# Fewer filler matmuls in the prologue, one shared ring for the mixed inputs, and a fourth output buffer

## The chip, the cores and the metric

The kernel runs on one core of a Trainium2 chip. Times are device microseconds of one execution. Eight runs of the kernel before gave 412.10 to 415.53 us, with a median of 412.3 us. A profile is one further execution, recorded by the hardware profiler; all readings of engines, waits and transfers below come from it.

## The reference

Two layers follow each other. The first is a causal convolution along the sequence with 7 taps per head (8 heads of 24 channels, taps from a softmax). The second is a channel mix: each position is blended with the position before it, in two ways, and the blends go through matrices.

```python
# x: (8, 4160, 192), weight: (8, 7)
w = softmax(weight, axis=-1)                       # per head
y = sum over k of w[h, k] * x_padded[s + k]        # causal, pad 6 zeros in front
y_prev = y shifted by one position
xk = mu_k * y + (1 - mu_k) * y_prev
xr = mu_r * y + (1 - mu_r) * y_prev
k = relu(xk @ w_k)                                 # (.., 1024)
v = (k * k) @ w_v                                  # (.., 192)
out = sigmoid(xr @ w_r) * v                        # float32
```

## The kernel before

The eight sequences are worked on in four pairs; 64 channels of one sequence and 64 of the other fill the 128 partitions. A pair's positions are cut into steps, mostly of 512 positions (three steps of 256 at the very start, one of 256 at the end of the first pair, and one that collects the tails of all pairs). Each step of 512 has eight "slots" of K work. Four slots make a bundle, and a bundle is the unit of the order, which is written out by hand: `manual_schedule` keeps the instructions of each engine as the Python code issues them.

**Prologue** (lines 824 to 867). The taps' weights are loaded and put through a softmax on ScalarE and VectorE; the first block of x comes in through two hardware queues into `x_f` and is cast into `xb`; GpSimd issues the other loads of x and of the matrices. TensorE meanwhile runs matmuls whose results nobody reads: `SHORT` = 85 matmuls of one column (line 851), three of 512 columns (line 822, `WARM[0]`), then, after the eight small matmuls of the taps (line 254), two more of 512 columns. The first useful convolution matmuls follow at line 413 (`conv_t`), as soon as `xb` is cast.

**First bundles** (`bundle_first`, `bundle_second`, `bundle_third`). These turn the convolution of the first positions straight into the transposed layout `yT`, while K's matmuls for the three short steps start. The order on TensorE is: 168 matmuls of line 413, four slots of K (line 593), one slot, and then, between more slots and convolutions, slots 4 and 5 of the short steps. The third bundle begins with K's matmuls for two slots, followed by R's (line 650) and V's (line 681).

**Steady state** (`bundle_rest`). In each bundle TensorE computes four K slots, R for 256 positions and V for 256 positions, and a convolution unit for later positions. ScalarE applies the relu (line 605) and the sigmoid (line 661) out of PSUM, VectorE squares K (line 619), forms the difference `d` (line 536), scales and adds it into `xk` and `xr` (lines 567 and 573, function `scale`, `add_y`, `mix`) and multiplies V by R into `o_sb` (line 697, `v_out`). SyncE issues two stores per `o_sb`, and the writes and transposing reads of `y`.

**Buffers.** A tile pool gives each tag a ring of buffers. A tile takes a buffer that is free, and its first writer waits for the last reader of the tile that held it. K's inputs `xk` and R's inputs `xr` have three buffers each, of 128 partitions by 3 x 512 bf16; `o_sb` has three of 128 by 768 float32; `k_sb` has four. PSUM is one ring of four tiles of two banks.

In a step of 512, whose slots fill bundles f and f+1, `xk` is first written in bundle f-1 and last read by the last slot of bundle f+1; `xr` is first written late in bundle f-1 and last read by R's second half in bundle f+3.

The built program has 15,465 TensorE instructions in a row, a weight load and a matmul each for 7,718 matmuls and a few others; the TensorE has no loop.

Of the kernel before, what the change touches and what calls it, by code (L numbers as in the profile page):

```python
# [7 lines left out]
FP32 = mybir.dt.float32  # L8
BF16 = mybir.dt.bfloat16
# [5 lines left out]
def kernel(  # L15
# [13 lines left out]
    B, S, D = x.shape  # L29
# [3 lines left out]
    P = 128  # L33
    NF = DF // P
    Q = 64
    NC = D // Q
# [8 lines left out]
    STEP = 512  # L45
# [1 line left out]
    NPAIR = B // 2  # L47
    YC = 16
    WARM = (3, 2)
    SHORT = 85  # L50

    const = ctx.enter_context(tc.tile_pool(name="const", bufs=1))
    two = ctx.enter_context(tc.tile_pool(name="two", bufs=2))
    three = ctx.enter_context(tc.tile_pool(name="three", bufs=3))
    four = ctx.enter_context(tc.tile_pool(name="four", bufs=4))
    ring = ctx.enter_context(tc.tile_pool(name="ring", bufs=4, space=bass.MemoryType.PSUM))
    dram = ctx.enter_context(tc.tile_pool(name="dram", bufs=1, space=bass.MemoryType.DRAM))

# [457 lines left out]
    diffs, xks, xrs = {}, {}, {}  # L516
# [5 lines left out]
    def y_of(s, cs, k):  # L522

        p, t0, L, _, _ = steps[s]
        if s == LAST:
            return y_tail[:, cs, :, k : k + TAIL, :].rearrange("p c a t b -> p c a (t b)")
        return yTs[p][:, cs, YC + t0 - 1 + k : YC + t0 - 1 + k + L]
# [12 lines left out]
    def mix(s, i, sl=slice(0, NC)):  # L540

        L = steps[s][2]
        d = diffs[s]
        if s < 2 and i == 0:
            if sl.start == 0:
                xks[s] = three.tile([P, NC, STEP], BF16, tag="xk", name="xk")
            t = xks[s]
            c = sl.start
            nc.vector.scalar_tensor_tensor(  # L549
                out=t[:, c, :L],  # L550
                in0=d[:, c, :L],
                scalar=mu[:, i, c : c + 1],
                in1=y_of(s, sl, 0)[:, 0, :],
                op0=ALU.mult,
                op1=ALU.add,
            )
            return
        scale(s, i, *range(sl.start, sl.stop))
        add_y(s, i, sl)

    def scale(s, i, *cs):
        L = steps[s][2]
        if s not in (xks, xrs)[i]:
            (xks, xrs)[i][s] = three.tile([P, NC, STEP], BF16, tag=("xk", "xr")[i], name=("xk", "xr")[i])
        t = (xks, xrs)[i][s]
        for c in cs:
            nc.vector.tensor_scalar(  # L567
                out=t[:, c, :L], in0=diffs[s][:, c, :L], scalar1=mu[:, i, c : c + 1], scalar2=None, op0=ALU.mult
            )

    def add_y(s, i, sl=slice(0, NC)):
        o = shaped(s, (xks, xrs)[i][s][:, sl, : steps[s][2]])
        nc.vector.tensor_tensor(out=o, in0=o, in1=y_of(s, sl, 0), op=ALU.add)  # L573
# [57 lines left out]
    def v_mm(o, s, t):  # L631
        for f in range(NF):
            nc.tensor.matmul(  # L633
                out=o,
                lhsT=k2s[s][:, f, t * P : (t + 1) * P],
                rhs=wv[:, f, :],
                start=(f == 0),
                stop=(f == NF - 1),
            )
# [51 lines left out]
    def tile_of(s, j, k):  # L691
        return k // 2 * (steps[s][2] // P) + 2 * j + k % 2

    def v_out(s, j):
        p, t0, L, _, _ = steps[s]
        o_sb = three.tile([P, 4, D], FP32, tag="o_sb", name="o_sb")
        nc.vector.tensor_tensor(  # L697
            out=o_sb.rearrange("p (b t) d -> p b (t d)", b=2),
            in0=v_ps.pop((s, j)),
            in1=r_sbs.pop((s, j)),  # L700
            op=ALU.mult,
        )
        for st in range(2):
            c = t0 + 2 * j * P
            nc.sync.dma_start(
                out=out[2 * p + st, c : c + 2 * P, :].rearrange("(m p) d -> p m d", p=P),
                in_=o_sb[:, 2 * st : 2 * st + 2, :],
            )

    def v_last(s, j):  # L710

        r_sb = r_sbs.pop((s, j))
        o_sb = three.tile([P, 4, D], FP32, tag="o_sb", name="o_sb")
        for k in range(4):
            ps = ring.tile([P, 2, BANK], FP32, tag="k", name="ps_v")
            v_mm(ps[:, 0, 0:D], s, tile_of(s, j, k))
            nc.vector.tensor_tensor(
                out=o_sb[:, k, :],
                in0=ps[:, 0, 0:D],
                in1=r_sb[:, k // 2, k % 2 * D : (k % 2 + 1) * D],  # L720
                op=ALU.mult,
            )
            (nc.scalar if k % 2 else nc.sync).dma_start(
                out=bass.AP(
                    tensor=out.tensor,
                    offset=out.offset + ((4 * (k % 2) + k // 2) * S + T0) * D,
                    ap=[[D, TAIL], [2 * S * D, 2], [1, D]],
                ),
                in_=o_sb[:, k, :],
            )  # L730
# [49 lines left out]
    for s, (p, t0, L, n0, ns) in enumerate(steps):  # L780
        fb = first_bundle[s]
        if s == 0:
            at(mix_a, 1, mix, s, 1)
            continue
        if s < 3:
            at(late, s + 1, mix, s, 1)
        else:
            if s == 3:
                at(mix_c, 1, diff, s)
            elif s == 5:  # L790
                at(mix_b, fb - 1, diff, s)
            else:
                at(mix_c, fb - 2, diff, s)
            at(mix_b if s == 5 else mix_a, fb - 1, scale, s, 0, 0)
            at(mix_b, fb - 1, scale, s, 0, 1, 2)
            at(mix_c, fb - 1, add_y, s, 0)
            if s == 3:
                at(mix_a, fb, scale, s, 1, 0)
                at(mix_b, fb, scale, s, 1, 1)
            else:  # L800
                at(mix_c, fb - 1, scale, s, 1, 0)
                at(mix_a, fb, scale, s, 1, 1)
            at(mix_b, fb, scale, s, 1, 2)
            at(mix_b, fb, add_y, s, 1)
        if s == LAST - 1 or s < LAST and steps[s + 1][0] > p:
            at(late, fb - 1, keep_tail, p)
# [17 lines left out]
    def prologue():  # L824
# [23 lines left out]

        for i in range(SHORT):
            q = slice(i % 4 * 32, i % 4 * 32 + 32)  # L850
# [18 lines left out]
    def bundle_first(ns):  # L869
        new_yT(0)  # L870
        tiles = [ring.tile([P, 2, BANK], FP32, tag="k", name="ps_t") for _ in range(2)]
        for n, (g, c) in enumerate((g, c) for g in range(2) for c in range(NC)):
            o = tiles[n % 2][:, n // 2 % 2, :]
            conv_t(g, c, o, range(groups[g][2]))
            if n == 0:
                turn_mu()
            to_yT(g, c, o, 0, groups[g][2], nc.scalar.copy)
            if g == 0:
                diff(0, slice(c, c + 1))
                if c == 0:  # L880
                    nc.vector.tensor_copy(out=mu.rearrange("p i c -> p (i c)"), in_=warm_ps[:, 1, 0 : 2 * NC])
                mix(0, 0, slice(c, c + 1))

        for c in range(NC):
            diff(1, slice(c, c + 1))
            mix(1, 0, slice(c, c + 1))
        diff(2)
        mix(2, 0)
        for n in ns:
            k_mm(n)  # L890
            k_relu(n)
        for n in ns:
            k_square(n)
        run(late, 0)
# [32 lines left out]
    def bundle_rest(b, ns):  # L927
# [3 lines left out]
        if b == 3:  # L931
            for n in range(2):
                k_mm(ns[n])
                k_relu(ns[n])
            tr(3, 0)
            tr(3, 1)
            k_square(bundles[b - 1][3])
            for u in xt[b - 1]:
                conv_tiles(*u)
                conv_tiles_out(*u)  # L940
            run(mix_a, b)
        else:
            if b == 4:
                v_out(*vq[b - 1][0])
            k_square(bundles[b - 1][3])
            run(mix_a, b)
            if b > 4:
                v_out(*vq[b - 1][0])
            for n in range(2):
                k_mm(ns[n])  # L950
                k_relu(ns[n])
# [26 lines left out]
    def bundle_third(b, ns):  # L978

        quad = vq[b][0]  # L980
        for n in bundles[b - 1][2:]:
            k_square(n)
        run(mix_a, b)
        k_mm(ns[0])
        k_relu(ns[0])
        k_square(ns[0])
        k_mm(ns[1])
        k_relu(ns[1])
        run(rq, b)
        run(rs, b)  # L990
        v_rows(*quad, 0)
        conv_out(*xt[b - 1][1], nc.scalar.copy)
        k_square(ns[1])
        run(mix_b, b)
        run(mix_c, b)
        run(late, b)
        k_mm(ns[2])
        k_relu(ns[2])
        v_rows(*quad, 1, (0,))
        k_mm(ns[3])  # L1000
        k_relu(ns[3])
        v_rows(*quad, 1, (1,))
        v_out(*quad)
        k_square(ns[2])
# [56 lines left out]
```

## Time and profile before

| what | value |
|---|---|
| median of 8 runs | 412.3 us |
| profiled execution's own time | 412.14 us |
| its span, first to last instruction | 410.4 us |
| TensorE busy (matmuls) | 401.4 us, 98% |
| VectorE busy | 372.2 us, 91% |
| ScalarE busy | 354.6 us, 86% |
| share of TensorE in the chain that ended last | 93% |
| packets of the instruction queue q8 | 60, 0.98 MB together |

Busy time of TensorE comes from records whose ends are modelled, so that matmuls in a row overlap in the records; idle time before a group is the safer reading. "PEld" is TensorE loading weights, "issue" is time in which an engine waited for nothing that the profile shows. In the rows of the chain of waits the columns are the start in microseconds, the length and what ran; in those of groups by line they are the line, the engine, the operation, the tiles, shapes and count, then busy time, the mean time of one in nanoseconds, and the idle time ahead of it with what ended it. In the rows of waits, the total, the number of times and the longest are given. In the rows of queues the number of packets, the megabytes and the share of 16 engines are given.

### The profile page before, as it was taken

What the parts mean: (1) busy time and instruction counts of PE and PEld (TensorE: products, weight loads), DVE (VectorE), ACT (ScalarE), POOL (GpSimd) and SP (SyncE); (2) the same over time, 40 slices, a digit from 0 to 9 for tenths busy, and PEclk for the clock granted to TensorE, in tenths of its full rate; (3) what the DMA queues carried; (4) which work ended last, traced back from release to release, by engine and by line L of the source; (5) the groups of instructions that cost most, each with busy time, mean ns of one, the idle gap of its engine ahead of it and who ended that gap; (6) DMA issues with size and microseconds to landing.
All of it is one profiled execution on the core that took longest, in us unless ns stands there. A gap on an engine that the chain in (4) does not pass through costs nothing.

```text
span 410.4 us, 17521 instructions
## 1 busy us (share of the span) xinstructions
PE 401.4 (98%) x7718; PEld 304.6 (74%) x7718; DVE 372.2 (91%) x680; ACT 354.6 (86%) x426; POOL 58.1 (14%) x91
## 2 busy tenths in 40 slices
PE   7889999999999999999999999999999999999996
PEld 5676777777877777767777777777777778777795
DVE  5989899998989999989999999999999899999973
ACT  6888988898998789988898998889898878887781
POOL 8623023030051003204020022100000001000000
PEclk9999999999999999999999999999999999999999
DMA  8999889998569997999995996968633846221223
GB/s 144 191 201 188 180 192 213 238 200 211 133 106 221 203 235 122 217 221 179 217 134 152 241 158 143 171 166 207 126 94 85 214 134 156 81 68 50 80 78 117
DMA packets 139124, 66.36 MB, mean 162 GB/s; under 512 B 89364, under 2 KB 139048, under 8 KB 139048
## 3 DMA queue, kind: packets, MB, share of 16 engines
q1 hardware_dynamic: 95704, 48.32, 46.7%
q0 software_dynamic: 42544, 16.36, 34.6%
q8 instruction: 60, 0.98, 1.0%
q10 hardware_dynamic: 800, 0.57, 0.5%
q14 instruction: 16, 0.13, 0.1%
HBM read 33.29 MB, written 36.99 MB: 171 GB/s over the span
## 4 chain that ended last, share of the span: by engine, by line
PE 93%; DVE 4%; DMA 1%; issue 1%; ACT 1%; ACTq 0%
PE ps_v L681 41%; PE ps_k L593 39%; PE ps_r L650 8%; PE ps_c L364 2%; PE ps_v L633 1%; PE ps_t L413 1%; DVE k L619 1%; DMA x_f<-in_x_dram 1%; PE ps_c L319 1%; DVE d L536 1%; DVE xr L567 0%; DVE xk L549 0%; DVE yT L511 0%; PE ps_c L393 0%; ACT k_sb L605 0%
## 5 line engine op out<-in xcount | busy, mean ns | idle before, releaser
L605 ACT ACTIVATE k_sb<-ps_k 128x1024 bf16<-128x1024 f32 x260 | 253.3, 1040 | 35.1 <-PE ps_k L593 34.7
L619 DVE TENSOR_TENSOR k<-k_sb 128x1024 bf16<-128x1024 bf16 x260 | 173.2, 686 | 25.1 <-ACT k_sb L605 25.0
L593 PE MATMUL ps_k<-xk,wk 64*128 64x512 bf16 (+1 forms) x1680 | 192.0, 361 | 2.0 <-issue 1.1
L681 PE MATMUL ps_v<-wv,k 64*128 64x192 bf16 x4032 | 188.4, 243 | 0.0
L681 PEld LDWEIGHTS <-k 64*128 64x128 bf16 x4032 | 168.4, 94 | 12.0 <-issue 4.5
L593 PEld LDWEIGHTS <-wk 64*128 64x128 bf16 x1680 | 85.4, 94 | 56.6 <-issue 2.4
L154 POOL DMA_DIRECT2D xb<-in_x_dram x62 | 43.9, 716 | 143.6 <-DVE xb L125 59.6
L697 DVE TENSOR_TENSOR o_sb<-ps_v,r_sb 128x768 f32<-128x768 f32 x64 | 60.8, 950 | 2.6 <-issue 2.4
L661 ACT ACTIVATE r_sb<-ps_r 128x768 bf16<-128x768 f32 x65 | 53.7, 827 | 8.8 <-PE ps_v L681 7.2
L337 ACT CAST y<-ps_c 128x960 bf16<-128x960 f32 (+2 forms) x84 | 52.6, 709 | 0.0
L650 PEld LDWEIGHTS <-xr 64*128 64x128 bf16 x780 | 34.8, 94 | 14.6 <-issue 0.7
L650 PE MATMUL ps_r<-wr,xr 64*128 64x192 bf16 x780 | 43.2, 243 | 0.5 <-DVE o_sb L697 0.5
L567 DVE TENSOR_SCALAR xr<-d,mu 128x512 bf16<-128x512 bf16 (+1 forms) x105 | 35.4, 343 | 0.0
L567 DVE TENSOR_SCALAR xk<-d,mu 128x512 bf16<-128x512 bf16 (+1 forms) x99 | 32.7, 365 | 0.1
L536 DVE TENSOR_TENSOR d<-yT 128x1536 bf16<-128x1536 bf16 (+2 forms) x38 | 31.5, 829 | 1.3 <-ACT yT L423 1.2
L573 DVE TENSOR_TENSOR xr<-xr,yT 128x1536 bf16<-128x1536 bf16 (+1 forms) x34 | 31.2, 918 | 1.2
L573 DVE TENSOR_TENSOR xk<-xk,yT 128x1536 bf16<-128x1536 bf16 (+1 forms) x32 | 29.9, 934 | 0.1
L520 POOL COPY y_tail<-yT 128x195 bf16<-128x195 bf16 x4 | 3.4, 844 | 89.5 <-DMA yT<-y_dram 89.5
L364 PEld LDWEIGHTS <-toe 32*32 32x32 bf16 x640 | 4.4, 87 | 8.6 <-issue 7.4
L364 PE MATMUL ps_c<-xb,toe 32*32 32x240 bf16 x640 | 9.3, 267 | 0.0
L127 POOL MEMSET xb<- 32x384 bf16 x3 | 1.2, 408 | 55.2 <-DVE xb L125 48.6
L413 PEld LDWEIGHTS <-xb 128*32 128x32 bf16 (+3 forms) x264 | 4.9, 113 | 2.1 <-ACT xb L247 1.3
(58 smaller groups left out, 66.8 us busy)
## 6 DMA issues: line engine op xcount, KB each, us to landing
out_dram<-o_sb SPq DMA_DIRECT2D x128, 192.0 KB
xb<-in_x_dram POOLq DMA_DIRECT2D x52, 240.0 KB, 8.0
y_dram<-y SPq DMA_DIRECT2D x40, 195.0 KB
y_dram<-y SPq DMA_DIRECT2D x16, 210.0 KB
xb<-in_x_dram POOLq DMA_DIRECT2D x4, 228.0 KB, 5.0
xb<-in_x_dram POOLq DMA_DIRECT2D x4, 192.0 KB, 6.2
wk<-in_moe_w_k_dram POOLq DMA_DIRECT2D x4, 192.0 KB, 6.7
xb<-in_x_dram POOLq DMA_DIRECT2D x2, 216.0 KB, 4.8
```

The costliest lines, as they stand in the source:

```text
L154: nc.gpsimd.dma_start(out=xb[q0 : q0 + rows, lo:hi, s, :], in_=bass.AP(tensor=x.tensor, offset=x.offset + (b * S + t0 + lo * step) * D, ap ...
L337: nc.scalar.copy(out=bass.AP(tensor=y.tensor, offset=y.offset + d, ap=[y.ap[0], [m * 2 * D, 2], [2 * D, m], [Q, 2], [1, b - a]],), in_=bas ...
L536: nc.vector.tensor_tensor(out=shaped(s, diffs[s][:, cs, :L]), in0=y_of(s, cs, 1), in1=y_of(s, cs, 0), op=ALU.subtract)
L567: nc.vector.tensor_scalar(out=t[:, c, :L], in0=diffs[s][:, c, :L], scalar1=mu[:, i, c : c + 1], scalar2=None, op0=ALU.mult)
L573: nc.vector.tensor_tensor(out=o, in0=o, in1=y_of(s, sl, 0), op=ALU.add)
L593: nc.tensor.matmul(out=ps[:, i, f * L : (f + 1) * L], lhsT=wk[r, c, fs], rhs=xk[r, c, :L], start=c == 0 and f == 0, stop=c == NC - 1 and f ...
L605: nc.scalar.activation(out=k_sb, in_=ps.rearrange("p a b -> p (a b)"), func=AF.Relu)
L619: nc.vector.tensor_tensor(out=o, in0=i, in1=i, op=ALU.mult)
L650: nc.tensor.matmul(out=ps[:, i, k * D : (k + 1) * D], lhsT=xr[q, c, ts], rhs=wr[q, c, :], start=c == 0, stop=c == NC - 1,)
L661: nc.scalar.activation(out=r_sbs[s, j], in_=r_ps.pop((s, j))[:, :, 0 : 2 * D], func=AF.Sigmoid)
L681: nc.tensor.matmul(out=v_ps[s, j][:, bank, k * D : (k + 1) * D], lhsT=k2s[s][q, f, t * P : (t + 1) * P], rhs=wv[q, f, :], start=half == 0 ...
L697: nc.vector.tensor_tensor(out=o_sb.rearrange("p (b t) d -> p b (t d)", b=2), in0=v_ps.pop((s, j)), in1=r_sbs.pop((s, j)), op=ALU.mult,)
```

## The change

`SHORT` goes from 85 to 60. The tags `xk` and `xr`, three buffers each, become one tag `xkr` with five. `o_sb` moves from a ring of three to a ring of four. The pool with five buffers is new.

```diff
-    SHORT = 85
+    SHORT = 60
...
+    five = ctx.enter_context(tc.tile_pool(name="five", bufs=5))
...
-                xks[s] = three.tile([P, NC, STEP], BF16, tag="xk", name="xk")
+                xks[s] = five.tile([P, NC, STEP], BF16, tag="xkr", name="xk")
...
-            (xks, xrs)[i][s] = three.tile([P, NC, STEP], BF16, tag=("xk", "xr")[i], name=("xk", "xr")[i])
+            (xks, xrs)[i][s] = five.tile([P, NC, STEP], BF16, tag="xkr", name=("xk", "xr")[i])
...
     def v_out(s, j):
-        o_sb = three.tile([P, 4, D], FP32, tag="o_sb", name="o_sb")
+        o_sb = four.tile([P, 4, D], FP32, tag="o_sb", name="o_sb")
...
     def v_last(s, j):
-        o_sb = three.tile([P, 4, D], FP32, tag="o_sb", name="o_sb")
+        o_sb = four.tile([P, 4, D], FP32, tag="o_sb", name="o_sb")
```

As built, TensorE has 50 instructions fewer (25 weight loads and 25 matmuls of line 851), and 15,415 in all. The order of everything else is the same on all five engines. On VectorE three waits of the mix differ. The first `xk` of a step of 512 no longer waits for TensorE; the `xr` of the second short step (written in the third bundle) and the first `xk` of the second pair now do. The waits of `o_sb` for stores name the store four tiles back instead of three.

## The prediction

> **What bounds the kernel now.** I read the engines' busy time first, then the chain of waits, then the groups that the edits touch, and last the instruction queue's packets.
>
> ```profile
> PE 401.4 (98%) x7718; PEld 304.6 (74%) x7718; DVE 372.2 (91%) x680; ACT 354.6 (86%) x426; POOL 58.1 (14%) x91
> PE 93%; DVE 4%; DMA 1%; issue 1%; ACT 1%; ACTq 0%
> ```
>
> TensorE bounds the span: it is 93% of the chain that ended last. Nearly all of VectorE's 4% lies before 38 us. So an edit is worth what it takes from TensorE's idle time or, ahead of 38 us, from this chain:
>
> ```profile
> 9.25 0.57 ACT yT L423
> 9.84 0.30 DVE d L536
> ...
> 18.12 0.76 PE ps_k L593 x12
> ...
> 20.24 0.11 PE ps_k L593 x2
> 20.35 1.07 issue
> 21.42 1.38 PE ps_k L593 x22
> ```
>
> One piece is odd: TensorE stands still for 1.07 us from 20.35 inside a slot of K, between two matmuls with the same operands, for "issue". It is the largest such piece in the chain. Now the prologue on TensorE:
>
> ```profile
> 1.53 0.83 PE L851 MATMUL warm<-ones_t 128*32 128x1 bf16 x85 [1.53 <-DVE ones_t L830]
> 2.30 1.46 PE L822 MATMUL warm<-zeros,ones_t 128*128 128x512 bf16 x3
> 4.23 0.35 PE L254 MATMUL w_ps<-w_tap,tap 8*128 8x8 bf16 x8 [0.47 <-DVE w_tap L252]
> 4.52 1.03 PE L822 MATMUL warm<-zeros,ones_t 128*128 128x512 bf16 x2
> 5.93 0.79 PE L413 MATMUL ps_t<-toe,xb 128*32 128x120 bf16 x24 [0.38 <-ACT xb L247]
> ```
>
> The 85 fillers end at 2.30; the taps' matmuls wait for VectorE until 4.23 and the convolution for ScalarE's cast until 5.93. VectorE's waits for its output tile over the whole run, and two queues in one microsecond ahead of the stall:
>
> ```profile
> DVE o_sb L697 <- issue: 2.4, 1, 2.4
> ...
> DVE o_sb L697 <- PE ps_v L681: 0.2, 1, 0.2
> ```
>
> ```profile
> q0 software_dynamic: 490, 0.18, 154.1%
> q8 instruction: 1, 0.02, 6.1%
> ```
>
> The last two are the window 18.5 to 19.5 us: q0, GpSimd's loads, takes the engines more than whole, and one instruction packet is among them. The page counts 60 such packets with 0.98 MB, 16,384 bytes each in the packet records, for 15,465 TensorE instructions: 256 instructions each (60 x 256 = 15,360). Counted in the built program, exactly 961 instructions stand before the idle's end. The first four packets start at 4.93, 12.76, 18.95 and 25.41 and take 0.94 to 0.97. So I read the idle as a wait for code: with blocks that begin at instructions 193, 449, 705, 961, 1217 and so on, the packet at 18.95 lands at 19.92 and the block runs at 21.42, 1.5 later. Each packet is asked for when the block before it is entered; at quiet times it starts 1.1 to 1.25 after the instruction some 60 places ahead of that entry has begun.
>
> **The change part by part.** The sum is made against the profiled execution's 412.14 (span 410.4, 1.7 around it), 0.16 under the median of 412.3.
>
> *The 25 matmuls.* 0.77 us for 85 (1.53 to 2.30) is 9 ns each, so 25 x 9 = 0.23 us. It is hidden: the taps' matmuls still wait for `w_tap` at 4.23, so the idle of 0.47 ahead of them becomes 0.70. Value 0. Cover gone would cost at most 0.23.
>
> *The ring of five.* In steady state a first write of `xk` finds live the last `xk`, the last `xr` and the `xr` before, then adds `xk` and `xr`: five. So none waits. The wait taken away (first `xk` of a step of 512, at 22.14) had VectorE busy until it: 0 gained. The two added waits are for the last slot of the second bundle (TensorE at 18.05 to 18.9, writer at 26.28) and for reads of the bundle before, which VectorE's square of that bundle's last slot has already outwaited. Behind a wait there would stand `k_square`, then the V matmuls. Value 0; bounds: VectorE's idle before the `xk` and `xr` rows, 0.0 and 0.1, below, and one slot of K, 1.3 (27.20 row, 12 matmuls of 109 ns), above.
>
> *The fourth output buffer.* `o_sb` has one idle of 2.4 at its first use, where no store has been issued, and 0.2 for TensorE. Nothing waits for stores. Value 0, at most 0.2 gained.
>
> *The 50 instructions fewer.* This moves all 59 block entries 50 instructions, 25 matmuls, later in the work. Nothing else of the change touches TensorE's path, so it carries the forecast. In the numbering of before, entries come at 243, 499, 755, 1011, 1267.
>
> First the chain that sets 961 today. Entry 449 is foreseen at 8.67; packet at 12.76 (4.1 later), usable 0.97 + 1.48 later at 15.2; that sets off the packet at 18.95 (3.75 later), usable at 21.42; that one the packet at 25.41 (3.99), usable at 27.85, when 1217 runs with nothing to spare. So in this stretch of full q0 a block needs 6.2 to 6.5 us, and TensorE is held at this pace.
>
> After: entry 499 is foreseen at 9.28 instead of 8.67. If its own block is there by then, 9.28 + 6.5 = 15.8 (755 is reached at 16.1), + 6.2 = 22.0 for 1011, which ran at 22.72 before: 0.7 gained. Had the delay been nothing, 1.07 would be.
>
> But is the block of 499 there? Its packet is asked for by entry 243, foreseen 60 places ahead, at the taps' matmuls: 3.7 to 4.2, against 2.0 today. Today's started 2.9 after. The nearest rows for one with q0 active are 3.75 to 4.1. I take 3.4, halfway: 4.0 + 3.4 + 0.95 + 1.5 = 9.85. That is 0.55 after 9.28, so the chain slips: 16.4, 22.55 for 1011, and 0.16 gained. Ends: 3.7 + 2.9 + 2.4 = 9.0 (0.7 gained, at most 1.07) and 4.2 + 4.1 + 2.4 = 10.7 (0.7 lost).
>
> *The other 55 entries.* Without stall today, but two of them with under 0.5 us to spare (at 71.5 and 163.1). Drawing the delays of like places for the moved entries gives 0.2 lost on average, 0 to 0.7 in most draws. I take 0.2.
>
> Sum: 412.14 + 0 + 0 + 0 - 0.16 + 0.2 = 412.2.
>
> [...]
>
> **The rivals.**
>
> *The stall goes.* If the first packet is early, 0.7 to 1.07 is gained and no other entry stalls: 411.1 to 411.4. For it: q0 begins only at 4.0, so little may stand ahead of the packet. Against it: all saturated rows.
>
> *The first packet comes late, slower than before.* If the foreseeing stops at an instruction that waits, entry 243 is only seen after 5.93, when `xb` is cast (four instructions of the convolution's first 24 stand at 6.0 to 6.5). Then 6.1 + 3.9 + 2.4 = 12.4 for 499, 18.9 for 755, 25.1 for 1011, against 22.72: +2.4, 414.5. It decides by over 0.3% once block 499 is usable after 11.2 (9.28 + 0.7 + 1.24). Against it: today's first packet starts 0.7 after the wait at 4.23 ends, less than the 1.1 of any quiet one, so it was asked for before.
>
> [...]
>
> *It does nothing.* The stall only moves and keeps its 1.07: 412.1, in my range anyhow.
>
> **How the numbers follow.** The likeliest (stall kept in part, 411.5 to 413.0) has 0.55. The stall gone has 0.20; with luck at other entries a part of it passes 0.3%, which is 1.24 us and about what a measurement of this kernel can tell from no change. The late packet has 0.15, its smaller versions among them; the clock 0.05; several late stalls at other entries, each up to 1 us, 0.05. Faster by over 0.3% (under 411.06): 0.12. Slower (over 413.54): 0.22, from the last three less their small cases. Same: 0.66. The range runs from 410.9, the whole stall gone and 0.2 more, to 414.2, most of the late packet's case.
>
> **What would show it.** Right: `o_sb`, `xk` and `xr` rows without new idle; line 851's group ends near 2.08 with 0.7 idle ahead of line 254; the "issue" piece of 20.35 is gone from its place, and one stands, if any, in R's matmuls of line 650 (instruction 1011) near 21.5, shorter than 1.07; the first q8 packet starts near 7.4. Wrong: an "issue" idle of over 0.5 near 10 us in line 413, or the first packet after 9; "issue" in later bundles at block edges; line 413 slow beyond 9.4.

## The result: 0.5% slower, and the profile after

The changed kernel takes 414.94 us (median of 25 runs, 413.54 to 417.37) against 412.83 us (67 runs): a ratio of 1.0051, 95% interval 1.0041 to 1.0061, or 2.1 us. Forecast were 412.2 us and "same". The profiled execution took 413.86 us, near the low end of the 25, with a span of 412.1 us: 1.7 over the profile before.

The page of the changed kernel, busy time of the engines and the chain that ended last, looks much as it did:

```profile
PE 402.5 (98%) x7693; PEld 305.6 (74%) x7693; DVE 372.7 (90%) x680; ACT 354.9 (86%) x426; POOL 59.1 (14%) x91
PE 92%; DVE 2%; issue 0%; ACTq 0%
```

This chain reaches back only to 21.2 us, so it does not hold the stretch that the forecast was about. I went there. TensorE's instructions of the changed kernel in order of time (start, length, line, tiles, count, and in brackets the idle ahead and what ended it):

```profile
1.53 0.62 PE L852 MATMUL warm<-ones_t 128*32 128x1 bf16 x60 [1.53 <-DVE ones_t L831]
2.09 1.46 PE L823 MATMUL warm<-zeros,ones_t 128*128 128x512 bf16 x3
4.24 0.36 PE L255 MATMUL w_ps<-w_tap,tap 8*128 8x8 bf16 x8 [0.69 <-DVE w_tap L253]
...
5.55 0.79 PE L414 MATMUL ps_t<-toe,xb 128*32 128x120 bf16 x24
...
6.47 3.35 PE L414 MATMUL ps_t<-toe,xb 128*32 128x120 bf16 x124
11.85 0.44 PE L414 MATMUL ps_t<-toe,xb 128*16 128x120 bf16 x20 [2.03 <-issue]
12.21 5.77 PE L594 MATMUL ps_k<-xk,wk 64*128 64x256 bf16 x72
17.91 1.02 PE L414 MATMUL ps_t<-toe,xb 128*32 128x120 bf16 x64
...
24.59 0.58 PE L651 MATMUL ps_r<-wr,xr 64*128 64x192 bf16 x9 [0.78 <-issue]
```

All lines are one higher than before, for the line that the new pool adds. The fillers' part went as forecast: 0.62 us for 60, and 0.69 idle ahead of the taps. New is an idle of 2.03 us for "issue" inside line 414, where TensorE's chain of 168 convolution matmuls had run unbroken. It ends at instruction 449 of the built program, 256 after 193, the first edge of a block of code. The idle of 1.07 us at 20.35 is gone; in its place, at instruction 961 again but 25 matmuls later in the work, stands one of 0.78.

The queues say why. From 4.5 to 9.5 us, the kernel before and then the changed one (packets, megabytes, share of 16 engines):

```profile
q0 software_dynamic: 1339, 0.71, 111.9%
q8 instruction: 1, 0.02, 1.2%
```

```profile
q0 software_dynamic: 1302, 0.70, 117.3%
q1 hardware_dynamic: 13, 0.00, 0.4%
```

GpSimd issues the same loads; the instruction packet is missing from the second. In the packet records it starts at 9.54 instead of 4.93 and ends at 10.51, and its block runs at 11.85. From there the edges follow each other much as before, one per 5.6 to 6.7 us:

| edge, instruction | reached, before | idle there | reached, changed | idle there |
|---|---|---|---|---|
| 449 | 9.39 | none | 11.85 | 2.03 |
| 705 | 15.80 | none | 18.40 | none |
| 961 | 21.42 | 1.07 | 24.59 | 0.78 |
| 1217 | 27.85 | none | 31.25 | none |

The changed kernel's edges stand 25 matmuls later in the work, so its 24.59 compares with 22.72 before: 1.87 late. The first V matmuls of the third bundle come at 24.93 instead of 23.25, and the last group of all at 402.89 instead of 401.15: 1.68 and 1.74. Little is lost or won between. The stretch of 345 us from 43.3 before and from 45.0 now shows the same work on every engine, 6,534 and 6,533 matmuls. So this pair of profiles accounts for 1.7 of the 2.1 us between the medians.

The idle is followed by half clock. Windows of the changed kernel, three, and then the middle one of the kernel before. After the busy time and count of the five engines come the clock that TensorE was granted, the busy share of the DMA engines and GB/s:

```profile
9.40:12.70 3.30, 1.27 (x53) 0.92 (x44) 1.54 (x5) 0.95 (x3) 2.65 (x5) 1.00 1.42 177
12.80:16.10 3.30, 3.30 (x36) 2.38 (x32) 3.08 (x8) 2.50 (x4) 2.69 (x4) 0.50 1.46 198
16.20:19.60 3.40, 3.40 (x108) 2.70 (x104) 3.07 (x6) 3.37 (x4) 0.71 (x1) 0.99 1.59 187
```

```profile
12.80:16.10 3.30, 2.98 (x77) 2.29 (x75) 3.27 (x8) 3.30 (x5) 2.63 (x4) 1.00 1.45 190
```

In 9.40 to 12.70 TensorE was busy 1.27 of 3.30 us; in the next window it was granted half its clock. K's matmuls there take 398 ns instead of 269:

```profile
L594 PE MATMUL ps_k<-xk,wk 64*128 64x256 bf16 x36 | 3.8, 398 | 0.0
```

In this execution that costs little by itself: the block of the next edge was usable at about 18.1 (the packet's end at 16.72 and 1.4), and TensorE came to it at 18.40, so some 0.3 us. Nor would an earlier packet alone have gained anything here: at half clock TensorE would still have come to the edge at 18.40. The late block and the half clock lie on top of each other at this edge.

### The profile page after: what moved, and what is told of

The parts are those of the page before. It is cut to its first block, busy times and chain, and to the rows that moved or that the text cites. A ratio compares the mean times of both kernels' runs of the same rounds, so it can differ in the third digit from the quotient of the medians.

```text
span 412.1 us, 17469 instructions
## 1 busy us (share of the span) xinstructions
PE 402.5 (98%) x7693; PEld 305.6 (74%) x7693; DVE 372.7 (90%) x680; ACT 354.9 (86%) x426; POOL 59.1 (14%) x91
## 4 chain that ended last, share of the span: by engine, by line
PE 92%; DVE 2%; issue 0%; ACTq 0%
PE ps_v L682 40%; PE ps_k L594 39%; PE ps_r L651 8%; PE ps_c L365 2%; PE ps_v L634 1%; PE ps_c L320 1%; DVE k L620 1%; DVE xr L568 0%; DVE yT L512 0%; DVE xr L574 0%; PE ps_c L394 0%; DVE o_sb L698 0%; DVE d L537 0%; PE ps_t L503 0%; DVE o_sb L718 0%
## 5 line engine op out<-in xcount | busy, mean ns | idle before, releaser
L594 PEld LDWEIGHTS <-wk 64*128 64x128 bf16 x1680 | 86.6, 95 | 54.6 <-issue 1.0
L521 POOL COPY y_tail<-yT 128x195 bf16<-128x195 bf16 x4 | 4.4, 1107 | 87.6 <-DMA yT<-y_dram 87.6
L414 PE MATMUL ps_t<-toe,xb 128*32 128x120 bf16 (+3 forms) x264 | 6.2, 262 | 2.0 <-issue 2.0
```

Source lines behind the costliest of these rows:

```text
L594: nc.tensor.matmul(out=ps[:, i, f * L : (f + 1) * L], lhsT=wk[r, c, fs], rhs=xk[r, c, :L], start=c == 0 and f == 0, stop=c == NC - 1 and f ...
```

## The experiments

Theory, after the result: the loss is late code. The first request for a block leaves TensorE later, and meets GpSimd's loads. Rivals: the buffers; the clock, through fewer fillers; and, inside the theory, what holds the request.

| kernel | median us | ratio to before, 95% | first q8 packet | idle for issue near 10 us, at 961 |
|---|---|---|---|---|
| changed | 414.94 | 1.0051 (1.0041 to 1.0061) | 9.54 | 2.03, 0.78 |
| 60 fillers alone | 415.01 | 1.0046 (1.0030 to 1.0062) | 9.52 | 1.93, 0.75 |
| rings alone, 85 fillers | 412.49 | 0.9992 (0.9977 to 1.0006) | 4.38 | none, 1.49 |
| 25 fillers moved behind the taps | 414.86 | 1.0049 (1.0031 to 1.0067) | 8.53 | 1.65, 1.32 |
| 25 fillers moved ahead of the taps | 412.62 | 1.0011 (0.9994 to 1.0028) | 6.76 | 0.07, 1.19 |
| 80 fillers | 412.96 | 0.9996 (0.9979 to 1.0012) | 6.50 | none, 0.53 |
| 76 fillers | 412.47 | 0.9993 (0.9984 to 1.0002) | 7.11 | none, 0.40 |
| 72 fillers | 416.15 | 1.0074 (1.0048 to 1.0099) | 10.39 | 2.20, 0.85 |
| 64 fillers | 415.24 | 1.0053 (1.0034 to 1.0072) | 10.98 | 2.63, 0.51 |
| changed, fewer loads | 412.80 | 0.9987 (0.9967 to 1.0008) | 9.51 | 1.61, 0.33 |
| changed, first x only | 411.30 | 0.9975 (0.9956 to 0.9993) | 7.05 | none, 0.49 |
| before, later loads | 412.39 | 0.9991 (0.9975 to 1.0006) | 5.41 | none, 0.69 |
| changed, once more | 414.24 | 1.0037 (1.0023 to 1.0052) | 9.77 | 1.95, 0.78 |

The ratios are to runs of the kernel before on the same chip.

### One part at a time

```diff
 # the kernel before
-    SHORT = 85
+    SHORT = 60
```

> The kernel before with 60 fillers and nothing else. Theory (late code): all of the loss is the 50 instructions, so it runs as the changed kernel does, 2.1 us over the kernel before (ratio 1.0051), with the first q8 packet at about 9.5 us and an idle of some 2 us for issue in the convolution matmuls at about 10 us. Rival (buffers): the shared ring or the moved tiles cost the time; then this one stands within 0.5 us of the kernel before.

```diff
 # the changed kernel
-    SHORT = 60
+    SHORT = 85
```

> The changed kernel with 85 fillers: the ring of five and the fourth output buffer alone. Late code: as the kernel before, within 0.3 us, with the idle of 1.07 us at 20.35 us in its place and the first q8 packet at 4.9 us. Buffers: 1.5 to 2 us slower than the kernel before.

The fillers alone give the whole loss (1.0046), the rings alone none (0.9992). TensorE's idle in the second says the same: 1.49 us at its old place and none near 10.

### The fillers, put elsewhere

```diff
 # the changed kernel (60 fillers), in the prologue
         softmax()
         warm(warm_ps, WARM[1])
+        for i in range(25):
+            q = slice(i % 4 * 32, i % 4 * 32 + 32)
+            nc.tensor.matmul(
+                out=warm_ps[q, 0, 0:1], lhsT=ones_t[:, 0:32], rhs=ones_t[:, 0:1], start=True, stop=True
+            )
```

> The changed kernel, with the 25 fillers that it lacks put in again, not ahead of the taps' matmuls but behind the last two matmuls of 512 columns, just ahead of the first convolution. The program has the same number of instructions ahead of each block's edge as the kernel before, while the fillers at the start stay 60. Late code: as the kernel before, within 0.4 us (the 25 take 0.23 us, in an idle of 0.38 us). Rival (fillers and clock): what counts is TensorE's activity before the taps' matmuls, so it stays 1.5 to 2 us slower.

The time was a miss for the theory, and this is the most useful run. All block edges stand where they do before, and it is as slow as the changed kernel. So where the edges fall is not enough. The first packet starts at 8.53; TensorE's rows:

```profile
4.24 0.36 PE L255 MATMUL w_ps<-w_tap,tap 8*128 8x8 bf16 x8 [0.69 <-DVE w_tap L253]
...
5.49 0.35 PE L861 MATMUL warm<-ones_t 128*32 128x1 bf16 x25
...
11.31 1.36 PE L414 MATMUL ps_t<-toe,xb 128*32 128x120 bf16 x45 [1.65 <-issue]
```

By itself it also fitted the clock rival. Its complement, run later, has the same 25 three lines up:

```diff
 # the changed kernel (60 fillers), in the prologue
         warm(warm_ps, WARM[0])
+        for i in range(25):
+            q = slice(i % 4 * 32, i % 4 * 32 + 32)
+            nc.tensor.matmul(
+                out=warm_ps[q, 0, 0:1], lhsT=ones_t[:, 0:32], rhs=ones_t[:, 0:1], start=True, stop=True
+            )
         x_tile(2)
         softmax()
```

> The changed kernel, with the 25 fillers put in again behind the first three matmuls of 512 columns and ahead of the taps' matmuls, so before the wait that ends at 4.2 us (the earlier run had them behind it). Theory (the request for the second block goes out with the instruction some 20 places ahead of the edge, and is late when that one stands behind a wait): that instruction is now one of the moved fillers, issued at about 3.6 us; the first q8 packet starts at 5 to 7 us, no idle for issue at 10 us, and the time is that of the kernel before, within 0.5 us. Rival (what counts is TensorE's activity before 3.5 us, so the clock): 1.7 to 2.1 us slower, as with the fillers moved behind the taps.

Now the fillers run at 3.48, ahead of the wait for the taps, and the time is that of the kernel before:

```profile
3.48 0.35 PE L858 MATMUL warm<-ones_t 128*32 128x1 bf16 x25
4.24 0.36 PE L255 MATMUL w_ps<-w_tap,tap 8*128 8x8 bf16 x8 [0.41 <-POOL band L289]
...
6.57 3.32 PE L414 MATMUL ps_t<-toe,xb 128*32 128x120 bf16 x144
```

Both kernels have the same instructions, counts and edges. Only the side of the wait that ends at 4.24 differs, and with it 2 us. That fits a request whose moment is set by what runs ahead of the first edge, and when. The clock rival in its first form (fillers before 3.5 us count) isn't refuted by this run alone, but the next ones do that: with 76 fillers full clock is recorded only from 12.68 us, later than the 9.41 of the changed kernel, and that execution took 412.23 us.

### How many fillers

```diff
 # the kernel before
-    SHORT = 85
+    SHORT = 80
```

Three more runs have 76, 72 and 64 in the same line.

> The kernel before with 80 fillers. The first edge then lies at instruction 203 in the numbering of before, just behind the first convolution matmul, which waits for the cast of x until 5.6 to 5.9 us. Theory (the request for code is held by the waiting matmul): the first q8 packet starts at 9.3 to 9.9 us, 4 us after that wait ends, TensorE stands still about 2.4 us for issue from about 9.5 us, and the time is 2 to 2.6 us over the kernel before. Rival (the request is made 60 instructions ahead, waits or not): it is asked for at 2.1 us as before, the packet starts at 4.9 to 5.2 us, and the time is that of the kernel before, within 0.4 us.

> The kernel before with 76 fillers. The instruction 20 places ahead of the first edge is then one of the last matmuls of the taps, issued at 4.3 to 4.5 us, ahead of the wait for the cast of x. Theory (some 20 places): the first packet starts at 6.3 to 8 us, the idle at 10 us is 0 to 0.5 us, and the time is within 0.7 us of the kernel before, while 72 fillers cost 3 us. Rival (under 12 places in that stretch): the instruction is a convolution matmul behind the wait, the packet starts at 9.5 to 10.5 us, and it is 2 to 3 us slower.

> The kernel before with 72 fillers. If the request runs about 60 places ahead: asked for at 2.0 us, packet at 4.9 to 6.5 us, the time of the kernel before within 0.5 us. If 20 to 32: the instruction that many places ahead is one of the taps' matmuls or one of the two matmuls of 512 columns behind them, at 4.2 to 4.7 us, the packet starts at 6.5 to 8.3 us, and TensorE stands still for at most 0.8 us near 10 us; the time lies between 0.3 us under and 1 us over the kernel before.

> The kernel before with 64 fillers. The run with 80 showed that a waiting convolution matmul does not by itself hold the request for code, and the run with the 25 fillers moved showed that the number of instructions ahead of the edge is not all either. New theory: the request goes out when the instruction some number of places ahead of the edge has been issued, and it is late when that one stands behind a wait. If the number is about 60, that one is still a filler here, the request goes out at 2.0 us, the first q8 packet starts at 4.9 to 6.5 us, and the time is that of the kernel before, within 0.5 us. If it is 20 to 32, that one is a convolution matmul behind the cast of x, the packet starts at 8.5 to 9.6 us, TensorE stands still for issue near 10 us, and the time is 1.5 to 2.2 us over the kernel before.

With 80 and 76 it is the time of the kernel before; with 72 it is 3 us slower, with 64 some 2. That is a step, within four fillers of 9 ns each. TensorE's waits with 76 and with 72 (total, times, longest):

```profile
PE ps_t L413 <- ACT xb L247: 0.9, 1, 0.9
...
PE ps_k L593 <- issue: 0.4, 1, 0.4
```

```profile
PE ps_t L413 <- issue: 2.2, 1, 2.2
...
PE ps_k L593 <- issue: 0.8, 1, 0.8
```

The first edge is always instruction 193. With 76 fillers the first convolution's weight load, which waits for the cast of x, is instruction 181; with 72 it is 173. With 76 the packet starts at 7.11, 0.7 after the convolution begins (6.42); with 72 it starts 4.0 after (10.39 and 6.36). That fits a request that goes out with an instruction ahead of the edge: at least 13 places, or it would stand behind the wait with 76 too, and at most 20, or it would stand ahead of it with 72. The step comes when that instruction falls behind the wait. In the two runs with the 25 fillers moved, the same place is a filler: at 5.6 us behind the taps, and at 3.6 us (or the first of the taps, at 4.24) ahead of them. The expectation for 72 ("at most 0.8 us", taps not the convolution) was a miss by that bound. With 64 "about 60 places" was a miss; "20 to 32" had the time right and the packet too early (8.5 to 9.6 expected, 10.98 measured). The run with 80 refutes that the waiting matmul next to the edge holds the request: the edge is behind it, and the packet starts at 6.50, 0.9 after the wait's end. Its rival had the time right, but the packet too early as well (4.9 to 5.2).

### Is it GpSimd's loads that delay the packet?

```diff
 # the changed kernel, in the prologue
-        load_x(2)
-        load_wk(DF // 2, DF)
+        nc.gpsimd.memset(xbs[2], 0.0)
+        nc.gpsimd.memset(wk[:, :, DF // 2 : DF], 0.0)
```

> The changed kernel without the loads of x for the third group and without the second half of K's matrix, which GpSimd fills with zeros instead (two parts of the input left out, so that the outputs are not the reference's). It takes away transfers of q0 between 5.5 and 10 us and leaves TensorE's instructions as they are. Theory (the packet waits behind GpSimd's transfers): the first packet starts before 8.5 us, against 9.5, and the idle at 10 us shrinks from 2.0 to under 1 us. Rival (the packet is late for a reason of its own): it starts at 9.3 to 9.7 us and the idle stays 2.0 us.

A miss on the packet: 9.51, the idle 1.61. The time came back to 412.8 all the same:

```profile
11.85 0.44 PE L414 MATMUL ps_t<-toe,xb 128*16 128x120 bf16 x20 [1.61 <-issue]
...
16.99 1.02 PE L414 MATMUL ps_t<-toe,xb 128*32 128x120 bf16 x64
...
23.22 0.58 PE L651 MATMUL ps_r<-wr,xr 64*128 64x192 bf16 x9 [0.33 <-issue]
```

With q0 nearly empty from 9 to 11 us (share 0.2 and 0.4 in the packet records, against 1.2 and 1.5) the second packet started 2.35 after its edge instead of 3.91. The clock was also not halved, and K's 72 matmuls ended at 17.0 instead of 17.9. So from the same 11.85 the edge at 961 is reached at 23.22 instead of 24.59, against 22.72 for the same work before. With the first idle still there, only some 0.5 us is left; the rest of the loss comes with what follows it, the late second block and the half clock. Both are gone here, so this run does not tell them apart.

What was left out here had been issued after 5.5 us, so at best just ahead of the request at 5.6 to 5.8. The loads issued before still ran on q0 until 9.6 us, and the packet starts just as they run out. The next run leaves out also what was issued from 4.2:

```diff
 # the changed kernel, in the prologue
-        load_wk(0, DF // 2)
+        nc.gpsimd.memset(wk, 0.0)
...
-        load_x(2)
-        load_wk(DF // 2, DF)
+        nc.gpsimd.memset(xbs[2], 0.0)
```

> The changed kernel without the loads of K's matrix and of x for the third group, which GpSimd fills with zeros instead (parts of the input left out, so that the outputs are not the reference's). The run before left the transfers that came after 5.5 us out and the first packet stayed at 9.5 us; this one also leaves out those between 4.2 and 5.5 us, which were issued ahead of the request at about 5.8 us. Theory (the packet waits for the transfers that were handed to the DMA engines before it): it starts at 6.8 to 8 us and the idle at 10 us is under 0.5 us. Rival (the delay has nothing to do with GpSimd's transfers): the packet starts at 9.3 to 9.8 us and the idle stays 1.5 to 2 us.

The packet starts at 7.05, 0.4 us after q0 has run empty, and the idle is gone. The queues from 6 to 10 us, and TensorE's convolution unbroken:

```profile
q0 software_dynamic: 169, 0.06, 12.7%
q8 instruction: 1, 0.02, 2.0%
```

```profile
6.57 3.99 PE L414 MATMUL ps_t<-toe,xb 128*32 128x120 bf16 x144
```

TensorE's program is that of the changed kernel to the instruction, with 60 fillers, and it takes 411.3 us, 0.25% under the kernel before (some of that may be K's matrix, whose transfers are left out). This closes the case against the clock in its first form and against the fillers as such: the same 60 are harmless when the packet finds the engines free.

### Later loads, for the idle that was there before

```diff
 # the kernel before: the fifth group's loads move from the prologue into bundle_second,
 # tied to VectorE's order as the later groups are; the sixth group's move one bundle on
-        x_tile(4)
-        load_x(4)
...
-        if g > 4:
+        if g > 3:
...
         act_, dve_ = nc.scalar.copy, nc.vector.tensor_copy
+        x_tile(4)
+        load_x(4)
...
-            b = {5: 1, 6: 3, 7: 7}.get(g)
+            b = {5: 2, 6: 3, 7: 7}.get(g)
```

> The kernel before with 85 fillers, in which GpSimd issues the loads of x for the fifth group only when VectorE has squared the first four slots (about 16.6 us instead of 13.4), and those for the sixth group one bundle later (about 22 instead of 18.7). If the idle of 1.07 us at 20.35 us is a block of code that waits behind GpSimd's transfers, the third packet starts at 16.3 to 17.5 us instead of 18.95, that idle is gone, and the time is 0.7 to 1.1 us under the kernel before. If the packet is late for a reason of its own, it still starts near 19 us and the time stays within 0.3 us. A later load that comes too late for its convolution (near 29.5 us) would show as a wait of TensorE on that load.

A miss: the third packet starts at 19.06, near the 19 of the rival, and the time stays (0.9991). The idle shrinks to 0.69 only because TensorE comes to the edge later; the block runs at 21.41, against 21.42 before. This neither shows nor refutes that the old idle is a wait behind GpSimd's loads: those issued by 13.1 us still filled q0 (a share of 1.6) until 19, so the edit did not free the queue ahead of the packet. A new wait of 0.6 us for ScalarE's convolution copies, near 280 us, appears in the profile too.

### A second profile of the changed kernel

> The changed kernel once more, for a second profile of it. Theory (the idle at 10 us also costs clock): the record of the granted clock shows full speed only after 9 us, and in this execution either a stretch of 3.4 us at half after the idle, or full speed that begins later than 12 us; an execution of the second kind takes over 414.3 us in its profile, one of the first 413.7 to 414.3 us. Rival (the clock plays no part): the time in the profile does not follow the record of the clock.

It was of the first kind again: full clock recorded from 10.00, half from 13.41 to 16.83, and 414.05 us. With only one kind seen this doesn't decide. In the slow kernels taken together the profiles' times go with the clock record: 413.85, 413.86 and 414.05 where a half stretch follows the idle (60 fillers); 414.51 (fillers behind the taps) where full clock begins only at 14.59; 415.29 (64) where the half stretch lasts to 17.80; and 415.90 (72) where full clock begins at 18.36. The runs of the changed kernel point the same way in part: twelve, the profiled one among them, have a mean granted clock of 0.994 to 0.996 and a median of 414.56 us; five have 0.992 and a median of 415.75. Half clock for 3.41 us takes 0.004 off the mean, so by this estimate those five had two such stretches. The others, at 0.998 to 1.000, range from 413.54 to 416.28. The idles differ too, so how much of the loss is clock stays open.

## Why the prediction was wrong, point by point

- **The 25 matmuls, 0 us: wrong in its reason.** The 0.23 us itself was hidden as said (0.62 us, then 0.69 idle). But the fillers had another part: with 85 of them, the instructions ahead of the first edge ran before the wait for the cast of x; with 60, some stand behind it.
- **Ring of five and output buffer, 0: right.** The run with them alone gives 0.9992. VectorE's rows in the changed kernel show no wait for a store ahead of `o_sb` and none of the mix:

```profile
L698 DVE TENSOR_TENSOR o_sb<-ps_v,r_sb 128x768 f32<-128x768 f32 x64 | 60.8, 950 | 3.3 <-issue 2.4 <-PE ps_v L682 0.9
L568 DVE TENSOR_SCALAR xr<-d,mu 128x512 bf16<-128x512 bf16 (+1 forms) x105 | 35.8, 347 | 0.0
L568 DVE TENSOR_SCALAR xk<-d,mu 128x512 bf16<-128x512 bf16 (+1 forms) x99 | 32.4, 358 | 0.1
```

- **The 50 instructions fewer, -0.16: the step that failed.** What was right: blocks of 256 (the idles end at instructions 449 and 961), the chain of edges, and the question whether the block of 499 is there. The term that failed is "I take 3.4, halfway: 4.0 + 3.4 + 0.95 + 1.5 = 9.85". With the request at 13 to 20 places it is 5.6 to 5.8 for the request and 3.7 to 3.9 for the delay; measured are the packet's start at 9.54, then 0.97 and 1.34 to the run: 11.85, 2 us later. The larger part is the request's time, 1.6 to 1.8 us. It came from "some 60 places ahead", read off later, quiet edges, where it fits; at the first edge the runs put it at 13 to 20, and that instruction stands behind the cast. Even the upper end, 10.7, was too low, and so was the bound on the loss. The sum also had no term for the clock after an idle.
- **The rival "the first packet comes late" is what happened.** It gave 12.4, 18.9 and 25.1 for the edges and 414.5 in all, at a chance of 0.15; measured were 11.85, 18.40 and 24.59, and 414.94. I held against it that today's packet starts 0.7 after the wait at 4.23. That only shows that the request precedes that wait, which fits 85 fillers and not 60. Its reason, that a waiting instruction stops the request, holds only for an instruction far enough ahead of the edge: with 80 fillers the one just ahead of it did not (packet at 6.50). And 414.5 was reckoned from a profile of 412.14; the profile after has 413.86.
- **The clock rival, at a chance of 0.05: the wrong way round.** Matmuls of line 413 took 304 ns each from 6 to 9.2 us and 218 from 9.6 to 10.3 in the profile before, in which full clock is recorded from 9.40; with the change it is recorded from 9.41. So the 25 fillers fewer did not put that step off, and no run shows a loss by a later step without the idle: with 76 fillers it came at 12.68, and that execution took 412.23 us. But the idle that the fewer fillers let in (2.03 us, and 1.93 with 60 fillers alone) was followed by 3.41 us at half clock.
- **Later entries, +0.2: wrong, 0 in this pair of profiles.** The same 345 us of work take the same time.
- **The range, 410.9 to 414.2, missed.** It was cut inside the late packet's own 414.5. The base moved as well: over 67 runs the kernel before has a median of 412.83, 0.5 above the one that the forecast started from, and the miss at the upper end is 0.7.

## What to carry to other kernels

TensorE's unrolled program was itself an input that was loaded here, in 60 packets of 16,384 bytes for 256 instructions each, and the first of them started at 9.54 us with GpSimd's loads and at 7.05 with most of the early ones left out. So an idle for "issue" between two like instructions is worth counting against the block edges. By the theory that these runs fit, what mattered for a block was when it was asked for: an instruction that seems to do nothing let the request leave before a wait and before the loads began, and the count of fillers acted as a step (76 took 412.47 us, 72 took 416.15), not as a slope. When a cost hinges on such a moment, the row to size it by is the one at that place, with the waits ahead of it, and not the average of quiet places later on.

## What the runs showed of the hardware

- The request for a block of code fits an instruction 13 to 20 places ahead of the first edge in the prologue, and one some 60 places ahead at quiet edges later (the earliest packets there start 1.0 to 1.25 us after it). Why the two differ wasn't tried.
- With 85 fillers the first packet of code started at 4.38 to 5.41 in three profiles. After an edge at which TensorE had stood for its block, the next packet started 3.6 to 4.3 us later where q0 was full, and 2.35 later where it was nearly empty. A block that TensorE stood for ran 1.3 to 1.6 us after its packet's end. In the changed kernel, leaving out loads issued from 5.5 us on did not bring the first packet forward (9.51 against 9.54); leaving out those from 4.2 us on did (7.05).
- In each profile here TensorE passed all but one or two of 60 edges without an idle for "issue"; at the others it stood for 0.1 to 2.6 us each, all in the first 27 us, where loads fill the engines (q0 has a share of 123.5% from 0 to 30 us in the profile before).
- An idle of 1.93 to 2.03 us in TensorE, after full clock had been recorded, was followed by 3.41 us at half its clock, in each of the three profiles with 60 fillers at the start, none put elsewhere, and all loads, and one of 2.63 us with 64 fillers. An idle of 1.61 us, with fewer loads, was not.
